# Rounding 64-bit weights to fp32 by an integer addition on GpSimd, in six steps where there were eight, with a new order of the whole program

## The chip, the core and the metric

The kernel runs on one core of a Trainium2 chip. A core has five engines that work side by side, each through its own queue of instructions in a fixed order: TensorE (PE in the profile, with PEld for its weight loads), VectorE (DVE), ScalarE (ACT), GpSimd (POOL) and SyncE (SP, which here only starts transfers). An instruction at the head of a queue that has to wait holds up all that stands behind it. The metric is the time of one execution in microseconds.

## The reference

The program computes attention with pooled queries, and then a feed-forward layer that takes the maximum of three products:

```python
q_pool = q.reshape(B, H, S // 2, 2, D).mean(axis=3)          # q, k, v: (8, 8, 1152, 64)
scores = np.matmul(q_pool, k.transpose(0, 1, 3, 2)) / np.sqrt(D)
scores = scores - np.max(scores, axis=-1, keepdims=True)
attn = np.exp(scores)
attn = attn / (np.sum(attn, axis=-1, keepdims=True) + 1e-09)
x = np.matmul(attn, v).transpose(0, 2, 1, 3).reshape(4608, 512)
h = np.maximum(np.maximum(x @ w1, x @ w2), x @ w3)           # w1, w2, w3: (512, 768)
out = h @ w_out                                              # w_out: (768, 512)
```

The four weight matrices arrive as 64-bit floats, because a 32-bit array was multiplied by a 64-bit scalar on the host. The engines work with 32 bits, so the kernel has to turn each weight into a pair of 32-bit numbers: a high part that TensorE can take in one pass, and a low part that holds the rest.

## The kernel before, in words

**Attention.** The work is cut into 64 units: eight batches, four pairs of heads, two halves of 288 pooled queries. Of a unit d, PE makes nine blocks of scores (`pqk`, lines 441 and 442, four matmuls each, split in high and low queries). ACT copies each block to SBUF (`s`, line 447), and DVE keeps a running maximum of it (`acc`, lines 453 and 456). PE turns the maximum round (`pmt`, line 489), DVE reduces it (`m`, line 495), PE spreads it over the partitions (`pmb`, line 502), DVE subtracts it (line 517), and ACT takes the exponential (line 523). POOL adds up the nine blocks of the exponential (`ksum`, lines 536 and 538). PE multiplies by the values (`pav`, line 556) and sums over the keys (`psum`). A reciprocal (DVE, line 577) and a product (POOL line 580, `xr`) normalise. ACT and POOL then split the result into `xh` and `xl` (lines 644 and 647). For the keys and queries, POOL does the preparation (lines 323, 330, 337).

**Feed-forward.** After the eight units of a batch come 3456 / 8 = 432 matmuls against the three input matrices (`ph`, line 788) and 144 against the output matrix (`po`, line 844). The maximum of three is taken on DVE (`hm`, line 808), and split by ACT and POOL (`h_hi`, `h_lo`). PE runs these matmuls between the attention units of the next batches: they fill it where a unit has to wait.

**Converting the weights.** There are 24 pieces of 128 x 512 weights: 18 for the input matrices, 6 for the output matrix. Each is loaded (line 691) into one of two halves of a buffer `w64` as pairs of 32-bit words, the low word first; so each word is read with a stride of 8 bytes. Eight steps on three engines follow, written as `rebias` to `total` (lines 693 to 725): ACT rebuilds the exponent, DVE puts the sign and upper bits together in two steps, DVE takes out the power of two and scales the low word with it in two more, ACT rounds to the high part, POOL subtracts it, and POOL adds the scaled low word. A piece waits for the buffer half that the piece two before it used; the single scratch tile `w_m` goes from one piece to the next when the step `rest` is done. The converted weights of the input matrices are also stored for the later batches (line 728). The first batch's `ph` needs the 18 pieces one after the other; its first `po` needs all 24, and all of `h_hi` and `h_lo` (the list `hdone`, line 853).

**The order.** Every step is put on a list with its engine, an estimated cost, what it depends on, and an urgency. `arrange` (line 106) then plays the list through with these costs, and takes on each engine the ready step with the lowest urgency. The urgency is the number of the unit plus an entry of the table `RANK` for the kind of step. The result is written out as the fixed order of each engine's queue, so the table and the costs decide only the order.

## Time and profile before

| what | value |
|---|---|
| median of 3 runs | 1508.67 us (1505.15 to 1516.34) |
| the profiled execution: span, first to last instruction (the page has no other time of it) | 1509.3 us |
| PE busy | 1437.4 us, 95% |
| POOL busy | 1133.2 us, 75% |
| DVE busy | 1085.3 us, 72% |
| ACT busy | 912.7 us, 60% |
| conversions, first to last instruction | 57 to 459 us |

The profile gives one execution. Its groups of instructions show the line of the kernel, the engine, the operation, the tiles (output, then inputs), the shape, the count, the busy time with the mean of one in ns, and then how long the engine was idle before them and who ended that. The ends of matmuls are modelled and overlap, so for PE a stretch with many matmuls in a row is a better price than the mean of one. `PEclk` is the clock that TensorE was granted, as a share of its full clock.

### The profile page before, as it was taken

Reading aid. Unit: us, or ns where it says so; the run is one execution under the profiler, and the core shown is the slowest. Engines: PE = TensorE matmul, PEld = TensorE weight load, DVE = VectorE, ACT = ScalarE, POOL = GpSimd, SP = SyncE. Lnnn points to the kernel's source line nnn. Section 1 sums busy time; section 2 is a strip of 40 time slices with the busy share of each in tenths; the row PEclk is TensorE's granted clock in tenths of the full one; section 3 lists DMA queues with packets and bytes.
Section 4 is the critical chain, followed back from the end, with each engine's and each line's share of the span. In section 5 each row is a group of like instructions: output and inputs, shape, how many; then the busy total and the mean of one; then the engine's idle time right before and its main releaser. Section 6 shows DMA issues by size and latency. Waiting matters only on the chain.

```text
span 1509.3 us, 28532 instructions
## 1 busy us (share of the span) xinstructions
PE 1437.4 (95%) x10640; PEld 1234.1 (82%) x10640; DVE 1085.3 (72%) x1417; ACT 912.7 (60%) x1508; POOL 1133.2 (75%) x867
## 2 busy tenths in 40 slices
PE   7889898989679999999999999999999999999999
PEld 6566676777448999898988888888888988889899
DVE  4889789999897754676668776877578776877310
ACT  4766666775566644565666665776566665666311
POOL 1899899998988547667978787887888787885610
PEclk7878999999869999999999999999999999999999
DMA  6565455565544554456545654565555664562141
GB/s 185 145 176 157 111 166 155 162 197 174 173 112 116 171 165 159 132 163 178 162 139 166 194 183 110 164 192 152 153 150 157 189 189 122 164 178 84 61 163 64
DMA packets 105273, 231.51 MB, mean 153 GB/s; under 512 B 14384, under 2 KB 80816, under 8 KB 95920
## 3 DMA queue, kind: packets, MB, share of 16 engines
q1 hardware_dynamic: 104560, 229.11, 51.7%
q8 instruction: 85, 1.39, 0.4%
q10 hardware_dynamic: 576, 0.59, 0.2%
q14 instruction: 52, 0.43, 0.1%
HBM read 135.27 MB, written 18.87 MB: 102 GB/s over the span
## 4 chain that ended last, share of the span: by engine, by line
PE 66%; POOL 2%; DVE 2%; DMA 1%; issue 1%; ACT 1%; SPq 0%; ACTq 0%; POOLq 0%; DVEq 0%
PE ph L788 26%; PE pav L556 12%; PE po L844 10%; PE pqk L441 7%; PE pqk L442 7%; PE pmt L489 2%; PE psum L570 2%; PE pmb L502 1%; POOL ksum L538 1%; DMA qq<-qraw 1%; POOL xl L647 0%; DVE acc L456 0%; ACT s L447 0%; DMA kraw<-in_kT_dram 0%; DVE w L702 0%
## 5 line engine op out<-in xcount | busy, mean ns | idle before, releaser
L538 POOL TENSOR_TENSOR ksum<-ksum,s 128x576 f32<-128x576 f32 x448 | 650.5, 1452 | 29.6 <-ACT s L523 6.6
L788 PE MATMUL ph<-xh,w 128*128 128x288 f32 x2304 | 532.1, 300 | 11.1 <-DVE hm L808 10.2
L447 ACT COPY s<-pqk 128x576 f32<-128x576 f32 x576 | 361.3, 638 | 127.1 <-PE pqk L442 116.1
L517 DVE TENSOR_TENSOR s<-s,pmb 128x864 f32<-128x864 f32 x384 | 394.4, 1045 | 37.4 <-PE pmb L502 37.3
L788 PEld LDWEIGHTS ph<-xh,w 128*128 128x128 f32 x2304 | 392.7, 189 | 20.4 <-DVE hm L808 12.3
L441 PE MATMUL pqk<-qq,kc 128*128 128x288 f32 x1152 | 358.1, 326 | 40.0 <-DVE acc L456 30.6
L456 DVE TENSOR_TENSOR acc<-acc,pqk 128x576 f32<-128x576 f32 x448 | 334.8, 747 | 85.0 <-ACT s L447 81.7
L523 ACT ACTIVATE s<-s 128x864 f32<-128x864 f32 x384 | 354.4, 929 | 56.7 <-DVE s L517 53.0
L788 PE MATMUL ph<-xl,w 128*128 128x288 f32 x1152 | 341.2, 296 | 0.0
L442 PE MATMUL pqk<-qq,kc 128*128 128x288 f32 x1152 | 333.9, 304 | 0.0
L556 PE MATMUL pav<-s,v 128*64 128x288 f32 x2304 | 308.4, 422 | 0.0
L441 PEld LDWEIGHTS pqk<-qq,kc 128*128 128x128 f32 x1152 | 226.3, 196 | 74.7 <-DVE acc L456 47.1
L556 PEld LDWEIGHTS pav<-s,v 128*64 128x64 f32 x2304 | 167.4, 142 | 120.3 <-issue 17.0
L442 PEld LDWEIGHTS pqk<-qq,kc 128*128 128x128 f32 x1152 | 228.5, 198 | 0.0
L788 PEld LDWEIGHTS ph<-xl,w 128*128 128x128 f32 x1152 | 218.0, 189 | 0.0
L536 POOL TENSOR_TENSOR ksum<-s 128x576 f32<-128x576 f32 x64 | 91.7, 1433 | 105.0 <-ACT s L523 101.3
L819 POOL TENSOR_TENSOR h_lo<-hm,h_hi 128x288 fp32r<-128x288 f32 x96 | 79.1, 827 | 100.4 <-ACT h_hi L816 100.4
L495 DVE TENSOR_REDUCE m<-pmt 96x3 f32<-96x384 f32 x128 | 69.5, 550 | 108.8 <-PE pmt L489 108.6
L808 DVE TENSOR_TENSOR hm<-hm,ph 128x288 f32<-128x288 f32 x192 | 86.1, 449 | 79.0 <-PE ph L788 77.5
L577 DVE RECIPROCAL rs<-rs 128x288 f32<-128x288 f32 (+1 forms) x64 | 96.3, 1505 | 56.5 <-ACT rs L574 54.7
L337 POOL TENSOR_TENSOR kraw<-kraw 128x1152 fp32r<-128x1152 f32 x31 | 83.0, 2678 | 51.3 <-DMA qraw<-in_qT_dram 25.8
L844 PE MATMUL po<-h_hi,wo_hi 128*128 128x288 f32 x384 | 115.9, 302 | 0.0
(55 smaller groups left out, 1467.8 us busy)
## 6 DMA issues: line engine op xcount, KB each, us to landing
w<-w_split SPq DMA_DIRECT2D x63, 1024.0 KB, 5.2
kc<-kraw SPq DMA_DIRECT2D x384, 96.0 KB, 2.3
qq<-qraw SPq DMA_DIRECT2D x252, 144.0 KB, 2.9
v<-in_vr_dram SPq DMA_DIRECT2D x32, 576.0 KB, 3.8
kraw<-in_kT_dram SPq DMA_DIRECT2D x31, 576.0 KB, 4.6
qraw<-in_qT_dram SPq DMA_DIRECT2D x31, 576.0 KB, 4.3
w<-in_win_dram SPq DMA_DIRECT2D x18, 512.0 KB, 6.1
w_split<-w SPq DMA_DIRECT2D x9, 1024.0 KB, 5.0
```

The lines of the kernel that those rows point to most:

```text
L441: nc.tensor.matmul(ps[:, h - hs[0], :QH], w, qq[:, 0, h], start=True, stop=False)
L442: nc.tensor.matmul(ps[:, h - hs[0], :QH], w, qq[:, 1, h], start=False, stop=True)
L447: nc.scalar.copy(o.s[kk // 3][:, kk % 3, slice(*hs)], o.ps[kk, hs][:, :, :QH])
L456: nc.vector.tensor_tensor(acc, acc, ps, op=ALU.max)
L517: nc.vector.tensor_tensor(s, s, o.pb[h][:, None, :QH].broadcast_to([P, 3, QH]), op=ALU.subtract)
L523: nc.scalar.activation(s, s, AF.Exp, scale=SCALE)
L536: vec[e].tensor_tensor(o.ksum, o.s[0][:, 0], x, op=ALU.add)
L538: vec[e].tensor_tensor(o.ksum, o.ksum, x, op=ALU.add)
L556: nc.tensor.matmul(o.pav[64 * h : 64 * h + 64, :QH], pr.v[:, kk, h], o.s[kk // 3][:, kk % 3, h], start=(kk == 0), stop=(kk == NK - 1),)
L577: nc.vector.reciprocal(o.rs, o.rs)
L788: nc.tensor.matmul(t.ps[:, :QH], w[:, a, kk], xx[:, kk, qs], start=(kk == 0 and i == 0), stop=(kk == 3 and i == 2),)
L844: nc.tensor.matmul(t.ps[:, :QH], ww[:, kk, ms], hh[:, kk, qs], start=(kk == 0 and i == 0), stop=(kk == 5 and i == 2),)
```

## The change

A double's upper word holds the sign, the exponent and 20 bits of the mantissa. Its lower word holds 32 more, of which fp32 has room for three. Before, the low word was scaled to its place and kept in full, to be added at the end. Now ACT reduces the low word to its upper three bits, rounded, by a product with 2^-29 into an integer (`third`); DVE assembles the upper word as before (`shift`, `sign`); POOL adds the two as 32-bit integers, so that a carry runs on into the exponent (`join`). This is the weight as fp32. ACT rounds it to the high part (`high`) and POOL subtracts that (`low`), now straight into its place. `power`, `rest` and `total` go. The scratch tile `w_m` is free for the next piece when `sign` is done. Two estimated costs are different, and all 43 entries of the table of ranks are new.

```diff
 RANK = {
-    "qk": -95.970825,
-    "cp": 3.506714,
...
+    "qk": -867.337398,
+    "cp": -1020.701831,
...
-            def power(e):
-                nc.vector.tensor_scalar(w_m.bitcast(U32), o.f, 0xFF800000, None, op0=ALU.bitwise_and)
-
-            def rest(e):
-                nc.vector.scalar_tensor_tensor(o.low.bitcast(F32), o.low, 2.0**-52, w_m, op0=ALU.mult, op1=ALU.mult)
+            def third(e):
+                nc.scalar.activation(o.low, o.low, AF.Copy, scale=2.0**-29)
+
+            def join(e):
+                vec[e].tensor_tensor(o.f, o.f, o.low, op=ALU.add)
...
             def low(e):
-                vec[e].tensor_tensor(o.ff, o.ff, o.hi, op=ALU.subtract)
-
-            def total(e):
-                vec[e].tensor_tensor(o.lo, o.ff, o.low.bitcast(F32), op=ALU.add)
+                vec[e].tensor_tensor(o.lo, o.ff, o.hi, op=ALU.subtract)
...
             a = cstep([("sp", 0.4)], load, [converted[j - 2]] if j > 1 else pairs[1].kmoved, size=512)
+            c = cstep([("act", 0.57)], third, [a])
             a = cstep([("act", 0.57)], rebias, [a, rested.get(j - 1)])
-            a = cstep([("dve", 0.8)], shift, [a])
-            a = cstep([("dve", 1.4)], sign, [a])
+            a = cstep([("dve", 0.75)], shift, [a])
+            a = rested[j] = cstep([("dve", 1.4)], sign, [a])
+            a = cstep([("pool", 1.26)], join, [a, c])
             c = cstep([("act", 0.57)], high, [a] + gone)
-            a = cstep([("dve", 0.85)], power, [a])
-            a = rested[j] = cstep([("dve", 0.85)], rest, [a])
-            c = cstep([("pool", 1.26)], low, [c, a])
-            converted[j] = cstep([("pool", 1.26)], total, [c, a])
+            converted[j] = cstep([("pool", 1.0)], low, [c])
```

In the changed kernel `third` is line 707, `join` line 710, `high` still line 719, `low` line 722, and the lines behind them have numbers lower by four.

The new order is seen best at two places. The first is PE's queue at the first matmul of the first batch's `po`. In the names, the first number behind `pqk` is the unit (counted from 0) and the second the block of scores; `po0_0_0` is the first group of `po` of batch 0. Before:

```order
L502 MATMUL pmb20_0_4320<-ident_94,m20_0_4305 128x96 x3
L502 MATMUL pmb20_1_4329<-ident_94,m20_1_4318 128x96 x3
L441 MATMUL pqk21_3_4336<-qq10_1_4081,kc10_1_3996 128x288
L442 MATMUL pqk21_3_4336<-qq10_1_4081,kc10_1_3996 128x288
L441 MATMUL pqk21_3_4336<-qq10_1_4081,kc10_1_3996 128x288
L442 MATMUL pqk21_3_4336<-qq10_1_4081,kc10_1_3996 128x288
L844 MATMUL po0_0_0_4346<-h_hi0_1674,wo_hi_103 128x288
L844 MATMUL po0_0_0_4346<-h_lo0_1675,wo_hi_103 128x288
```

And in the changed kernel, at the same matmul:

```order
L441 MATMUL pqk19_2_3967<-qq9_1_3737,kc9_0_3467 128x288
L442 MATMUL pqk19_2_3967<-qq9_1_3737,kc9_0_3467 128x288
L441 MATMUL pqk19_2_3967<-qq9_1_3737,kc9_0_3467 128x288
L442 MATMUL pqk19_2_3967<-qq9_1_3737,kc9_0_3467 128x288
L840 MATMUL po0_0_0_3976<-h_hi0_1681,wo_hi_103 128x288
L840 MATMUL po0_0_0_3976<-h_lo0_1682,wo_hi_103 128x288
L840 MATMUL po0_0_0_3976<-h_hi0_1681,wo_lo_104 128x288
```

The first `po` moves from behind block 3 of unit 21 to behind block 2 of unit 19. Counted over PE's whole queue ahead of it, there stand 772 `pqk` matmuls before and 696 now, 360 `pav` and 324, 126 `pmt` and 114, 126 `pmb` and 108, 6 of the `psum` of line 570 and 2, and all 432 `ph` of the batch in both.

The second place is POOL's queue at the last piece of the output matrix (`wo_lo` is its low half, `ksum19` the sum of unit 19's blocks). Before:

```order
L722 TENSOR_TENSOR w64_105<-w64_105,wo_hi_103 128x512
L538 TENSOR_TENSOR ksum19_4206<-ksum19_4206,s19_2_4054 128x576
L580 TENSOR_TENSOR xr_107<-xr_107,rs18_4246 128x288
L538 TENSOR_TENSOR ksum19_4206<-ksum19_4206,s19_2_4054 128x576
L725 TENSOR_TENSOR wo_lo_104<-w64_105 128x512
L538 TENSOR_TENSOR ksum19_4206<-ksum19_4206,s19_2_4054 128x576
L722 TENSOR_TENSOR w64_105<-w64_105,wo_hi_103 128x512
L725 TENSOR_TENSOR wo_lo_104<-w64_105 128x512
L536 TENSOR_TENSOR ksum20_4373<-s20_0_4140 128x576
```

And in the changed kernel:

```order
L710 TENSOR_TENSOR w64_105<-w64_105 128x512
L538 TENSOR_TENSOR ksum17_3860<-ksum17_3860,s17_1_3604 128x576
L722 TENSOR_TENSOR wo_lo_104<-w64_105,wo_hi_103 128x512
L710 TENSOR_TENSOR w64_105<-w64_105 128x512
L538 TENSOR_TENSOR ksum17_3860<-ksum17_3860,s17_1_3604 128x576
L722 TENSOR_TENSOR wo_lo_104<-w64_105,wo_hi_103 128x512
L538 TENSOR_TENSOR ksum17_3860<-ksum17_3860,s17_2_3706 128x576
```

The last piece is finished in the middle of unit 17's sum, where it was finished at the end of unit 19's. In the new order one sum stands between a piece's `join` (line 710) and its `low` (line 722), and in that time ACT has to do `high`. Counted over POOL's queue up to the last step of the last piece, there are 160 steps of sums before (20 of line 536, 140 of line 538) and 141 now (18 and 123), 11 of line 337 and 9, 11 of line 323 and 10, 11 of line 330 and 9, 3 of line 580 and none, 12 `h_lo` and 16 `xl` in both, and 48 steps of conversion in both. Counted over DVE's queue up to the last step of a conversion that ACT's last `high` needs, there are 168 maxima (lines 453 and 456) and 151, 40 of line 495 and 36, 120 of line 517 and 108, 19 of line 577 and 16, and 23 each of lines 707 and 710 that are not there any more. On ACT up to the last `high` there are 189 copies of scores and 172, 120 exponentials and 108, and 24 steps `third` that are new.

More of the change, by code (lines that the diff above doesn't have):

```diff
@@ L34 @@
 RANK = {
-    "qk": -95.970825,
-    "cp": 3.506714,
-    "mx": -112.160269,
-    "rows": -148.312644,
-    "red": 23.466841,
-    "bc": -142.276903,
-    "sub": 99.862451,
-    "exp": -189.653089,
-    "keys": 148.893694,
-    "av": 19.232023,
-    "xcopy": -206.02547,
-    "psum": 18.355097,
-    "eps": -181.047585,
-    "inv": 113.796689,
-    "xm": -22.916262,
-    "load": -43.210932,
-    "prep": 250.679273,
-    "move": 65.149737,
-    "split": -97.511902,
-    "ffn": -47.593054,
-    "rate": 0.801853,
-    "mm": 67.95383,
-    "fetch": -234.19152,
-    "evac": -68.37474,
-    "hhigh": 38.661498,
-    "hlow": -51.844784,
-    "conv": 191.981971,
-    "rate0": 3.325971,
-    "first_qk": 41.083979,
-    "first_cp": -105.959101,
-    "first_mx": 56.619279,
-    "first_sub": 16.712798,
-    "first_exp": 260.515882,
-    "first_keys": -71.869651,
-    "first_av": -60.410117,
-    "first_xcopy": 62.582893,
-    "first_psum": -24.318635,
-    "first_inv": -22.423915,
-    "first_xm": -3.450351,
-    "first_load": -260.256351,
-    "first_prep": 57.308365,
-    "first_move": -123.943607,
-    "first_split": 239.216553,
+    "qk": -867.337398,
+    "cp": -1020.701831,
+    "mx": -50.846032,
+    "rows": -2170.249061,
+    "red": -1970.271541,
+    "bc": -886.869509,
+    "sub": -48.271976,
+    "exp": -431.984861,
+    "keys": 698.07215,
+    "av": 20.89773,
+    "xcopy": -534.99975,
+    "psum": -1688.951079,
+    "eps": -2029.164301,
+    "inv": -1616.629935,
+    "xm": 1.735842,
+    "load": 842.07771,
+    "prep": 910.260987,
+    "move": -979.706926,
+    "split": -453.845754,
+    "ffn": -46.517946,
+    "rate": 0.839773,
+    "mm": 69.352276,
+    "fetch": -16.130968,
+    "evac": -1432.973336,
+    "hhigh": 304.771171,
+    "hlow": 664.388548,
+    "conv": 297.955587,
+    "rate0": 7.822039,
+    "first_qk": 270.235766,
+    "first_cp": -256.862538,
+    "first_mx": 744.663022,
+    "first_sub": 1436.30733,
+    "first_exp": 291.229,
+    "first_keys": 1508.105231,
+    "first_av": -87.174641,
+    "first_xcopy": 563.586725,
+    "first_psum": 726.316903,
+    "first_inv": 110.337379,
+    "first_xm": 482.800536,
+    "first_load": -828.565839,
+    "first_prep": 1745.538476,
+    "first_move": -984.902661,
+    "first_split": -1171.347816,
 }
```

## The prediction

> **What bounds the kernel now.** I read the slices of the page first, for where TensorE isn't full. The two rows are PE's busy share and its granted clock, in tenths, in 40 slices of 37.7 us:
>
> ```profile
> PE   7889898989679999999999999999999999999999
> PEclk7878999999869999999999999999999999999999
> ```
>
> Behind the twelfth slice everything is a 9; ahead of it PE has gaps, and the clock is low there too. The two weakest slices, the 11th and 12th (PE 6 and 7, clock 8 and 6), stand just ahead of that, from 377 to 453 us. So the second view is the instructions in order of time around 458 us, POOL and PE:
>
> ```profile
> 457.60 1.04 POOL L725 TENSOR_TENSOR wo_lo<-w 128x512 fp32r<-128x512 f32 x1
> ...
> 458.51 0.30 PE L844 MATMUL po<-h_hi,wo_hi 128*128 128x288 f32 x1
> ```
>
> POOL's last step of the last weight piece ends at 457.60 + 1.04 = 458.6 (spans on POOL are rough), and the first `po`, which needs all 24 pieces, starts at 458.5. That is the gate. The third view cuts the span there; its columns are the stretch and its length, then busy time of PE, PEld, DVE, ACT, POOL with their counts, clock, DMA share, GB/s:
>
> ```profile
> 49.00:458.50 409.50, 352.38 (x2436) 271.06 (x2436) 366.52 (x477) 266.39 (x417) 371.34 (x261) 0.89 0.55 158
> 458.50:1509.30 1050.80, 1044.95 (x7990) 930.74 (x7988) 695.59 (x906) 623.58 (x1057) 744.39 (x590) 1.00 0.51 151
> ```
>
> Behind the gate PE is busy for 1045.0 of 1050.8 us at full clock: that part is bound by PE's work, and no saving elsewhere shortens it. Ahead of it POOL is busy for 371.3 of 409.5 us (91%) and DVE for 366.5 (90%), and PE idles for 57.1 us. ACT, at 266.4, has room. The chain that ended last says who holds PE up there:
>
> ```profile
> 430.79 3.00 DVE w L702
> ...
> 443.75 1.04 DVE w_m L707
> ...
> 445.45 1.17 DVE w L710
> 446.64 0.64 ACT w_m L694
> ...
> 455.25 0.46 PE pmt L489 x3
> ...
> 468.05 0.64 PE psum L570 x4
> ```
>
> The conversion's DVE steps are on it, two of them those that go. The waits in 49 to 459 us agree (engine, line, what it waited for, us, times, longest):
>
> ```profile
> PEld pqk L441 <- DVE acc L456: 37.3, 47, 2.4
> PE pqk L441 <- DVE acc L456: 24.6, 35, 1.9
> ```
>
> PE waits for DVE's maxima, which stand in one queue with the conversion.
>
> So the time is the gate's time plus PE's work behind it. Of the profiled execution the page shows only its span, 1509.3 us; the median of the runs is 1508.67, 0.04% from it, and I make the sum against the span.
>
> **The change part by part: behind the gate.** In the new order 76 `pqk`, 36 `pav`, 12 `pmt`, 18 `pmb` and 4 `psum` matmuls that stood ahead of the first `po` stand behind it (counted in PE's two queues). The prices, from long stretches of the chain:
>
> ```profile
> 1417.82 4.37 PE pav L556 x36
> ...
> 1429.57 57.35 PE ph L788 x432
> ```
>
> A 288-column matmul takes 57.35 / 432 = 0.133 us, so 76 `pqk` are 10.1. A unit's 18 `pav` are 36 in the trace (two passes), 4.37 us, so two units are 8.7. Four groups of three `pmt` at 0.46 are 1.8; six groups of `pmb`, priced like them, at most 2.8; two units of `psum` at 0.64 are 1.3. Sum 24.7. PE's work behind the gate becomes 1050.8 + 24.7 = 1075.5 us, if PE stays as full there. The conversion, the only thing the change takes from these queues, is over by then. **The gate must come before 458.5 - 24.7 = 433.8 us, or nothing is won.**
>
> **Ahead of the gate: POOL.** Groups of POOL in 49 to 459 us (count, then busy time and mean ns of one):
>
> ```profile
> L538 POOL TENSOR_TENSOR ksum<-ksum,s 128x576 f32<-128x576 f32 x133 | 201.1, 1512 | 11.2 <-ACT s L523 5.1
> L536 POOL TENSOR_TENSOR ksum<-s 128x576 f32<-128x576 f32 x19 | 27.0, 1422 | 14.3 <-ACT s L523 14.2
> L722 POOL TENSOR_TENSOR w<-w,w 128x512 f32<-128x512 f32 x18 | 26.8, 1492 | 0.1
> L337 POOL TENSOR_TENSOR kraw<-kraw 128x1152 fp32r<-128x1152 f32 x10 | 26.7, 2671 | 5.6 <-DMA w<-in_win_dram 5.0 <-ACT kraw L333 0.6
> L725 POOL TENSOR_TENSOR w<-w 128x512 fp32r<-128x512 f32 x18 | 20.5, 1139 | 0.2
> L330 POOL TENSOR_TENSOR qraw<-qraw 128x576 fp32r<-128x576 f32 x10 | 16.2, 1618 | 3.3 <-ACT qraw L326 3.3
> L323 POOL TENSOR_TENSOR qraw<-qraw 128x576 f32<-128x576 f32 x10 | 14.4, 1442 | 1.1 <-DMA qraw<-in_qT_dram 1.1
> L722 POOL TENSOR_TENSOR w<-w,wo_hi 128x512 f32<-128x512 f32 x6 | 8.6, 1436 | 0.4 <-issue 0.4
> L725 POOL TENSOR_TENSOR wo_lo<-w 128x512 fp32r<-128x512 f32 x6 | 7.3, 1218 | 0.2
> L580 POOL TENSOR_TENSOR xr<-xr,rs 128x288 f32<-128x288 f32 x3 | 3.3, 1096 | 0.0
> ```
>
> Up to the last piece POOL has in the new order 17 sums less at 1.512 (25.7 us), 2 first sums at 1.422 (2.8), 2 of line 337 at 2.671 (5.3), 1 of line 323 (1.4), 2 of line 330 (3.2) and 3 of line 580 (3.3): 41.7 us. The conversion has 48 steps on POOL as before. They cost 26.8 + 8.6 + 20.5 + 7.3 = 63.2 us, 2.63 a piece. No row shows an integer addition on POOL. `join` reads and writes with a stride, as line 722 does in part; `low` writes without one, as line 725. Both lie by these rows between 1.14 and 1.49, so the sum moves by -8.5 to +8.4 us; I take one of each, no change. With every other microsecond unchanged the gate is at 458.5 - 41.7 = 416.8.
>
> A second term is the stretch that POOL and DVE cause each other. In 600 to 1400 us, where nothing is converted, the same sum on POOL takes
>
> ```profile
> L538 POOL TENSOR_TENSOR ksum<-ksum,s 128x576 f32<-128x576 f32 x265 | 378.2, 1428 | 15.3 <-ACT s L523 1.5
> ```
>
> 1.428 against 1.512: 133 x 0.084 = 11.2 us. The DVE steps that go swing likewise (min/median/max ns):
>
> ```profile
> L707 DVE TENSOR_SCALAR w_m<-w x24: 381/972/1687, 64.9 to 451.3; 128x512 uint32<-128x512 uint32 x24
> L710 DVE SCALAR_TENSOR_TENSOR w<-w,w_m x24: 693/1238/1807, 65.9 to 452.2; 128x512 f32<-128x512 uint32 x24
> ```
>
> A step of fixed shape that takes 0.38 or 1.69 us is waiting for something inside. Of the conversion's 96 DVE steps 48 stay, so I take half of the 11.2: 6 us (bounds 0 and 11). **Gate at 411.**
>
> The Trainium skill (SBUF — State Buffer, section "SBUF: two separate sides") says that VectorE and GpSimd share a pair of ports as an exclusive lock, taken for the whole instruction, and by VectorE only for operations with two SBUF inputs or in a two-port mode; the swing in the two rows above agrees with it. By that rule alone the relief goes with the steps that take the lock, and all of the conversion's do, so it gives the same half; without it the gate would be at 417 and the time 1492.
>
> **Ahead of the gate: DVE, ACT, PE.** Rows of the whole execution:
>
> ```profile
> L710 DVE SCALAR_TENSOR_TENSOR w<-w,w_m 128x512 f32<-128x512 uint32 x24 | 33.0, 1374 | 0.4
> L707 DVE TENSOR_SCALAR w_m<-w 128x512 uint32<-128x512 uint32 x24 | 24.9, 1038 | 0.3
> L517 DVE TENSOR_TENSOR s<-s,pmb 128x864 f32<-128x864 f32 x384 | 394.4, 1045 | 37.4 <-PE pmb L502 37.3
> L456 DVE TENSOR_TENSOR acc<-acc,pqk 128x576 f32<-128x576 f32 x448 | 334.8, 747 | 85.0 <-ACT s L447 81.7
> L447 ACT COPY s<-pqk 128x576 f32<-128x576 f32 x576 | 361.3, 638 | 127.1 <-PE pqk L442 116.1
> L523 ACT ACTIVATE s<-s 128x864 f32<-128x864 f32 x384 | 354.4, 929 | 56.7 <-DVE s L517 53.0
> L694 ACT ACTIVATE w_m<-w 128x512 f32<-128x512 f32 x24 | 16.3, 681 | 23.6 <-DVE w L710 17.4 <-POOL ksum L538 5.0 <-DMA w<-in_win_dram 1.2
> ```
>
> DVE loses 23 x 1.374 + 23 x 1.038 = 55.5 us of conversion, and by the order 17 maxima (12.7) and 12 subtractions (12.5): over 80 us, twice POOL's 41.7 (which puts DVE's own way to the gate under 378). So DVE, level with POOL before, no longer decides. ACT gets 24 `third`, by line 694's row 0.681 each, 16.3 us, and loses 17 copies (10.8) and 12 exponentials (11.1): 5.6 less. The ACT waits for `w_m` from line 710 (17.4) shorten, since `sign` now frees it; I cost that at nothing, ACT's 143 us of idle time covering it, and at 17 us were ACT full. The DMAs are the same in number and size; their places in SP's queue I cost at nothing, as POOL's rows show one wait for a weight load (5.0 us), and at another 5.0 if it comes twice.
>
> PE has 24.7 us less ahead of the gate, so at its old losses it would be there at 433.8, not at 411: 23 us of its losses must go. Those are 57.1 us idle, and 0.11 of 409.5, 45 us, of clock. The waits for DVE's maxima alone are 37.3 us on the weight loads (I take the 24.6 on the matmuls as the same moments), and the weak slices 11 and 12, where no `ph` is left and no `po` allowed, go when the gate comes earlier. I take it that they give the 23.
>
> **Sum.** 411 + 1075.5 = 1486.5, so 1486 us, 1.5% under the span.
>
> **The rivals.** A: PE keeps its losses. Its waits come from the round of copy, maximum and next block, which the change leaves; then the gate is at 425 to 440 and the time about 1509 (433.8 + 1075.5). For it: PE waits for a maximum, and not for a conversion step itself; against it: DVE at 90% now has a fifth less to do, and in the chain above the conversion's steps stand between the maxima. This is also how the change could do nothing it says: the steps saved were no one's wait.
>
> B: more comes than I count. POOL's 38.2 us of idle time are waits for ACT's exponentials, which wait for DVE; halved, the gate is at 392 and the time 1467.
>
> C: `join` is slow. If the integer path takes twice line 722's 1.49, 24 x 1.49 = 36 us more, and no stretch relief: gate 453, time 1528. It breaks even at 24 x 0.95 on top, a `join` of about 2.4 us. The Trainium skill (GPSIMD Engine Reference, section 4.1 "Engine selection") says that GpSimd adds 32-bit integers natively and exactly; no run here shows a duration, so it only lowers this chance.
>
> D, the other side by a new wait: POOL was asked for two steps in a row, with 0.9 us of idle time ahead of all 48 (the last figures of the four rows); now `low` waits for ACT's `high`, which waits for `join`, with one sum between. ACT's queue holds copies and exponentials there; if each of the 48 steps finds POOL waiting for one 0.93 us exponential, that is 45 us: gate 456, time 1531. Behind the blocked POOL stand the sums, and PE's `psum` waits for them. It breaks even from 23 / 48 = 0.5 us a step. For it: POOL is the fullest engine. Against it: a sum covers 1.5 us, and ACT has a third of its time free.
>
> **How the numbers follow.** A measurement of this kernel can tell about 1% (15 us) from no change. Forecast 0.50 (1475 to 1498, by the bounds of POOL's steps and of the stretch), B 0.12, A 0.20, D 0.11, C 0.07. Faster by over 1% is under 1494: B and seven eighths of the forecast, 0.56. Slower, over 1524: most of D and C, 0.14. The rest, 0.30, is A and the edges. The range leaves out the end of B below and the far ends of C and D above: 1460 to 1521. The forecast's own is 1475 to 1498.
>
> **What would show it.** First `po` near 411 us with units 19 to 21 behind it; PE over 99% busy from there; POOL's sums ahead of it nearer 1.47; `join` and `low` together near 2.6 us; PE's waits for line 456 ahead of the gate down by 20 us. It is wrong if the gate comes after 430 (A, or D if POOL idles ahead of line 722 for over 10 us, or C if line 710 is over 2.4), or if PE has gaps behind it: each 0.1 us in the 45 units behind it is 4.5 us.

## The result and the profile after

The changed kernel takes 1465.39 us (median of 4 runs, 1464.28 to 1467.21) against 1509.22 (4 runs, 1505.15 to 1516.34): a ratio of 0.971, 95% interval 0.968 to 0.974. The forecast was 1486. Sign and range (1460 to 1521) hold; the time lies outside the forecast's own 1475 to 1498, and the gain is 44 us where 23 were forecast.

The profiled execution has a span of 1465.4 us. PE's busy share and granted clock in 40 slices of 36.6 us:

```profile
PE   7789899999899999999999999999999999999999
PEclk7989899999899999999999999999999999999999
```

The weak slices 11 and 12 of before (PE 6 and 7, clock 8 and 6) are gone; one 8 is left of them. The instructions in order of time around the first `po`, POOL and PE:

```profile
396.26 1.04 POOL L710 TENSOR_TENSOR w<-w 128x512 uint32<-128x512 uint32 x1
...
397.92 0.29 PE L840 MATMUL po<-h_hi,wo_hi 128*128 128x288 f32 x1
...
398.66 1.29 POOL L722 TENSOR_TENSOR wo_lo<-w,wo_hi 128x512 fp32r<-128x512 f32 x1
```

The first `po` is at 397.92, and POOL's last step of the last piece begins 0.7 us behind it. So the gate isn't a wait for that step. The busy time of each engine in the stretches around the gate (columns as in the prediction; the first two rows are before's and after's first 49 us, the others after's):

```profile
0.00:49.00 49.00, 40.07 (x218) 32.30 (x219) 23.15 (x35) 22.71 (x35) 17.45 (x17) 0.79 0.64 169
```

```profile
0.00:49.00 49.00, 37.02 (x200) 30.32 (x200) 22.15 (x33) 21.34 (x32) 15.45 (x16) 0.79 0.60 158
49.00:397.92 348.92, 309.58 (x2269) 244.57 (x2267) 288.36 (x393) 253.12 (x406) 319.12 (x235) 0.92 0.59 172
397.92:1465.40 1067.48, 1062.91 (x8176) 949.07 (x8174) 726.44 (x944) 652.88 (x1096) 785.39 (x618) 1.00 0.51 153
```

The gate comes 60.6 us earlier, and 16.7 us more stand behind it (1067.5 for 1050.8): 43.9 us. Behind it PE is 99.6% busy (99.4% before). Ahead of it POOL is busy 319.1 of 348.9 us (91%, as before), DVE only 288.4 (83%, before 90%). Groups of POOL and of the conversion in after, in the 349 us ahead of the gate:

```profile
L538 POOL TENSOR_TENSOR ksum<-ksum,s 128x576 f32<-128x576 f32 x118 | 173.3, 1470 | 7.6 <-ACT s L523 3.7
L702 DVE SCALAR_TENSOR_TENSOR w<-w_m,w 128x512 uint32<-128x512 uint32 x24 | 36.3, 1511 | 0.5
L710 POOL TENSOR_TENSOR w<-w 128x512 uint32<-128x512 uint32 x24 | 26.8, 1117 | 1.3 <-DVE w L702 1.3
L722 POOL TENSOR_TENSOR w<-w,w 128x512 fp32r<-128x512 f32 x18 | 25.2, 1404 | 1.7 <-ACT w L719 1.7
L707 ACT ACTIVATE w<-w 128x512 uint32<-128x512 uint32 x24 | 16.7, 696 | 3.9 <-DMA w<-in_win_dram 3.9
```

`join` takes 1.12 us and `low` 1.40: 2.52 a piece for 2.63. POOL idles 1.7 us in all ahead of `low` in the input matrices. And the waits in that stretch (engine, line, what it waited for, us, times, longest):

```profile
PEld pqk L441 <- DVE acc L456: 18.3, 24, 3.2
PE pqk L441 <- DVE acc L456: 16.2, 20, 2.9
ACT w L719 <- POOL w L710: 13.8, 9, 3.5
...
PEld psum L587 <- POOL ksum L538: 6.3, 7, 1.5
...
PEld pmb L502 <- DVE m L495: 4.2, 7, 1.8
```

PE's wait for DVE's maxima is halved (37.3 to 18.3 us on the weight loads). ACT waits 13.8 us for `join`, a new wait. The chain that ended last, from 326 us on, shows who sets the pace now:

```profile
326.47 1.48 POOL ksum L538
328.03 1.74 POOL ksum L538
...
332.74 1.33 POOL w L722
334.07 1.00 POOL w L710
335.07 0.78 POOL ksum L538
336.43 1.32 POOL w L722
```

Here POOL's steps follow each other. The chain of before has such a row too (nine POOL steps, from 415.7 to 429.2 us), but beside it DVE's conversion steps, of which this stretch of after has none.

### The profile page after: what moved, and what is told of

Read it like the earlier page. It is cut to its first block, busy times and chain, and to the rows that moved or that the text cites. A ratio compares the mean times of both kernels' runs of the same rounds, so it can differ in the third digit from the quotient of the medians.

```text
span 1465.4 us, 28407 instructions
## 1 busy us (share of the span) xinstructions
PE 1409.5 (96%) x10640; PEld 1224.0 (84%) x10640; DVE 1036.9 (71%) x1369; ACT 927.3 (63%) x1532; POOL 1120.0 (76%) x867
## 4 chain that ended last, share of the span: by engine, by line
PE 77%; POOL 9%; issue 4%; ACT 4%; DVE 4%; DMA 2%; SPq 1%; POOLq 0%; ACTq 0%; DVEq 0%
PE ph L784 27%; PE pav L556 16%; PE po L840 10%; PE pqk L441 8%; PE pqk L442 8%; POOL ksum L538 5%; PE pmt L489 3%; PE psum L570 2%; PE pmb L502 2%; DVE acc L456 1%; ACT s L447 1%; ACT s L523 1%; DVE s L517 1%; POOL w L710 1%; POOL w L722 1%
## 5 line engine op out<-in xcount | busy, mean ns | idle before, releaser
L784 PE MATMUL ph<-xh,w 128*128 128x288 f32 x2304 | 525.6, 298 | 3.4 <-DVE hm L804 2.8
L447 ACT COPY s<-pqk 128x576 f32<-128x576 f32 x576 | 365.3, 638 | 129.1 <-PE pqk L442 113.4
L784 PEld LDWEIGHTS ph<-xh,w 128*128 128x128 f32 x2304 | 389.8, 188 | 10.3 <-issue 5.7
L441 PE MATMUL pqk<-qq,kc 128*128 128x288 f32 x1152 | 349.5, 318 | 33.4 <-DVE acc L456 25.9
L442 PE MATMUL pqk<-qq,kc 128*128 128x288 f32 x1152 | 329.7, 301 | 0.0
L441 PEld LDWEIGHTS pqk<-qq,kc 128*128 128x128 f32 x1152 | 223.0, 194 | 57.0 <-DVE acc L456 33.0
L556 PEld LDWEIGHTS pav<-s,v 128*64 128x64 f32 x2304 | 167.4, 140 | 119.0 <-issue 12.9
L442 PEld LDWEIGHTS pqk<-qq,kc 128*128 128x128 f32 x1152 | 224.5, 195 | 0.0
```

Of the source, the lines that this page charges most:

```text
L441: nc.tensor.matmul(ps[:, h - hs[0], :QH], w, qq[:, 0, h], start=True, stop=False)
L442: nc.tensor.matmul(ps[:, h - hs[0], :QH], w, qq[:, 1, h], start=False, stop=True)
L447: nc.scalar.copy(o.s[kk // 3][:, kk % 3, slice(*hs)], o.ps[kk, hs][:, :, :QH])
L556: nc.tensor.matmul(o.pav[64 * h : 64 * h + 64, :QH], pr.v[:, kk, h], o.s[kk // 3][:, kk % 3, h], start=(kk == 0), stop=(kk == NK - 1),)
L784: nc.tensor.matmul(t.ps[:, :QH], w[:, a, kk], xx[:, kk, qs], start=(kk == 0 and i == 0), stop=(kk == 3 and i == 2),)
```

## The experiments

Three readings had to be told apart. **One**: POOL's work sets the gate, and the new order puts less of it there; the DVE steps that go matter little. **Two**: DVE sets it as well, by the sheer time of the steps that go, or by what they do to POOL. **Three**: one half of the change, conversion or table, makes the whole gain.

All of this is read from the stretch from 49 us to the first `po`. Each kernel's window gives its length and the busy time of DVE and POOL in it; idle is the length less that. In a fence of an experiment the line numbers are its own, some higher than after's by the lines it adds. Each ratio is against the kernel before, run beside it (medians 1509.5 to 1511.3). The theories that an expectation names are those of its own text.

| kernel | median us | first po at | behind it | DVE busy, idle | POOL busy, idle |
|---|---|---|---|---|---|
| before | 1509.2 | 458.5 | 1050.8 | 366.5, 43.0 | 371.3, 38.2 |
| after | 1465.4 | 397.9 | 1067.5 | 288.4, 60.6 | 319.1, 29.8 |
| e1: new conversion, old table | 1505.1 | 450.1 | 1053.2 | 313.2, 87.9 | 358.0, 43.1 |
| e2: old conversion, new table | 1524.9 | 477.1 | 1048.6 | 363.9, 64.2 | 368.1, 60.0 |
| e3: after, two DVE steps more on a piece's own data | 1503.9 | 432.3 | 1066.7 | 333.1, 50.2 | 330.0, 53.3 |
| e4: after, one POOL step more | 1485.7 | 418.4 | 1069.0 | 290.8, 78.6 | 338.8, 30.7 |
| e5: after, two reductions more | 1469.8 | 397.5 | 1067.0 | 309.5, 39.0 | 320.3, 28.2 |
| e6: after, the two removed kinds of step again, on constants | 1508.9 | 442.4 | 1065.8 | 343.2, 50.2 | 332.2, 61.2 |
| e8: new conversion, old table but one entry | 1492.2 | 425.9 | 1063.9 | 297.9, 79.0 | 338.8, 38.1 |
| e9: after, one entry old | 1468.2 | 390.3 | 1078.0 | 278.6, 62.7 | 312.0, 29.3 |
| e11: after, four reductions more | 1498.9 | 432.0 | 1066.6 | 336.3, 46.7 | 320.4, 62.6 |
| e12: before without the two DVE steps | 1496.4 | 442.9 | 1052.1 | 314.9, 79.0 | 359.3, 34.6 |
| e13: after without `sign` | 1453.6 | 383.9 | 1068.1 | 254.6, 80.3 | 308.1, 26.9 |
| e14: after, a third of `low` on DVE | 1459.6 | 390.3 | 1066.9 | 287.2, 54.1 | 312.9, 28.4 |

One of e5's four runs took 2275 us, at a granted clock of 0.554 where the other three have 0.970 to 0.976; those three lie within 1466.2 to 1470.4, and e5's median and ratio are theirs.

### The two halves alone (e1, e2)

e1 has the new conversion with its dependences and estimated costs, and the old table; e2 the old conversion with the new table. Their core:

```diff
# e1: before, and
+            c = cstep([("act", 0.57)], third, [a])
...
+            a = rested[j] = cstep([("dve", 1.4)], sign, [a])
+            a = cstep([("pool", 1.26)], join, [a, c])
...
+            converted[j] = cstep([("pool", 1.0)], low, [c])
# e2: before, and
-    "keys": 148.893694,
+    "keys": 698.07215,
...
```

> The new six-step conversion and its costs, but the table of ranks of before; the first po stands in PE's queue behind 768 pqk matmuls, as before (772). Theory 1 (the steps saved on DVE and the stretch of POOL count by themselves, the order only puts less ahead of the first po): first po near 445 us, time about 1495 us, PE's work behind the first po about 1050 us. Theory 2 (the new table made the whole gain): time within 5 us of 1509. Theory 3 (the conversion made the whole gain): 1465 to 1472.

> The eight-step conversion of before with the new table of ranks; the first po stands behind 772 pqk matmuls, as before. Theory 1: no step is saved, so first po near 455 us and, if the new order fills PE better behind it (a batch took 168 us before and 166 in the changed kernel), a time of about 1500 us. Theory 2 (the new table made the whole gain): 1465 to 1475. Theory 3 (the conversion made the whole gain): 1509 within 5.

e1: ratio 0.996 (0.994 to 0.998). e2: 1.009 (1.008 to 1.011). By its time alone e1 lies within the 5 us of 1509 that the theory of the table asks for, but by that theory e2 would take 1465 to 1475, and it is slower than before; so none of the three fits both runs. Neither half makes the gain, and they do not add up to it: -6 and +14 us apart, against the kernel before beside them (1511.2), and -44 together. The windows ahead of the gate, of e1 and of e2:

```profile
49.00:450.10 401.10, 345.77 (x2443) 267.99 (x2441) 313.18 (x430) 277.37 (x442) 358.00 (x261) 0.89 0.56 161
```

```profile
49.00:477.10 428.10, 353.84 (x2437) 274.67 (x2436) 363.94 (x477) 269.04 (x417) 368.06 (x259) 0.88 0.52 150
```

In e1 DVE is busy 53 us less than before, but POOL only 13 less, and the gate moves by 8. In e2 the table, played through with the old conversion's steps, puts the first `po` behind 772 `pqk` as before, not behind 696, so the kernel doesn't have after's order. The order is made by table and steps together, and the two can't be taken apart by swapping the table. The next runs keep after's order and change one engine's load in it.

### POOL's load in the new order (e4)

A second integer addition on POOL for each piece, into a tile that nobody reads:

```diff
             def join(e):
                 vec[e].tensor_tensor(o.f, o.f, o.low, op=ALU.add)
+                vec[e].tensor_tensor(w_d.bitcast(U32), o.low, o.low, op=ALU.add)
```

> The changed kernel in its own order, with a second integer addition on POOL behind each join, written to a tile that nobody reads: 24 x 1.12 = 27 us more on POOL ahead of the first po. Theory 1 (POOL paces the way to the first po, 91% busy): first po 20 to 27 us later, time 1485 to 1492 us. Rival (PE's round of copy, maximum and next block paces, POOL has slack): under 8 us more.

Measured 1485.65 us, 0.984 (0.982 to 0.985), as reading one expected. The added steps and POOL's window:

```profile
L712 POOL TENSOR_TENSOR w_d<-w 128x512 uint32<-128x512 uint32 x23 | 26.9, 1170 | 0.0
```

```profile
49.00:418.40 369.40, 318.21 (x2257) 251.41 (x2256) 290.82 (x393) 252.18 (x403) 338.75 (x255) 0.89 0.56 161
```

POOL's busy time ahead of the gate rises by 19.6 us (319.1 to 338.8) and the gate moves by 20.5. Not all of the 26.9 us of additions shows there, since two sums and a `join` that stood in after's stretch fall outside this one, and `low` is shorter (1.31 us for 1.40). POOL's idle time stays at 30. What PE waits for changes too:

```profile
PEld psum L588 <- POOL ksum L539: 21.1, 13, 3.6
```

PE's wait for POOL's sums goes from 6.3 to 21.1 us. In the new order, with DVE's load as after has it, POOL paces, one for one.

### DVE's load in the new order (e3, e5, e6, e11)

e3 puts two steps of the removed kind behind `sign`, on the piece's own data:

```diff
             def sign(e):
...
+                nc.vector.tensor_scalar(w_d.bitcast(U32), o.f, 0xFF800000, None, op0=ALU.bitwise_and)
+                nc.vector.scalar_tensor_tensor(w_d, w_d, 2.0**-52, w_m, op0=ALU.mult, op1=ALU.mult)
```

> The changed kernel in its own order, with two further DVE steps per piece, of the forms of power and rest, written to a tile that nobody reads. They put 24 x 2.4 = 58 us back on DVE, and two operations per piece that POOL shares its ports with. Theory 1 (DVE had to be relieved before POOL could pace): DVE would be busy for 346 of the 349 us between 49 and the first po, so the first po moves by 20 to 45 us and the time is 1485 to 1510. Rival (the order alone moved the first po, DVE's steps were no one's wait): under 5 us more, 1465 to 1470.

Measured 1503.89 us, 0.995 (0.993 to 0.997), in the range expected, but not for one reason alone: these steps read what `join` writes, so POOL waits 10.3 us for them, a wait that neither kernel has. `join` also takes 1.521 us, for 1.117 in after, while the sums stay at 1.465.

```profile
L713 POOL TENSOR_TENSOR w<-w 128x512 uint32<-128x512 uint32 x24 | 36.5, 1521 | 13.5 <-DVE w_d L706 10.3 <-ACT kraw L334 1.6 <-ACT xr L566 0.4
```

e5, e11 and e6 are without that: their steps read a constant tile and write one that nobody reads. e5 adds two reductions (one input), e11 four, e6 the two removed kinds of step.

```diff
             def sign(e):
...
# e5, and e11 with range(4)
+                for i in range(2):
+                    nc.vector.tensor_reduce(w_e[:, i : i + 1], w_d, axis=AX.X, op=ALU.max)
# e6
+                nc.vector.tensor_scalar(w_e.bitcast(U32), w_d.bitcast(U32), 0xFF800000, None, op0=ALU.bitwise_and)
+                nc.vector.scalar_tensor_tensor(w_e, w_d, 2.0**-52, w_d, op0=ALU.mult, op1=ALU.mult)
```

> The changed kernel in its own order, with two reductions of a constant 128x512 tile on DVE per piece, right behind sign. Nobody reads their result, they hold nothing that another step waits for, and they have one SBUF input. By the 0.55 us of the reduction of line 495 they are some 1.2 us a piece, 29 us on DVE ahead of the first po. The run before with two further steps moved the first po by 34 us, but those read tiles that join and the next rebias had to wait for. Theory 1a (DVE's time itself is on PE's path): first po 10 to 25 us later, time 1476 to 1492. Theory 1b (what cost was POOL's stretch and the waits of join and rebias, not DVE's time): under 6 us more.

> As the run above, but the two DVE steps have the forms of the removed power and rest (a tensor_scalar, and a scalar_tensor_tensor with two SBUF inputs) on constant tiles, 0.38 + 0.69 = 1.07 us a piece where nothing disturbs them (the shortest of before). Theory 1b: the steps stretch to over 2 us a piece, POOL's sums ahead of the first po become longer by some 0.04 us each and the first po moves by 10 to 20 us, time 1476 to 1488. Theory 1a: the same as the run above within 5 us.

> The changed kernel in its own order, with four reductions of a constant tile per piece on DVE where the run with reductions had two: 24 x 4 x 0.67 = 65 us of DVE time, as much as the two steps with the forms of power and rest took (62.2 us, gate 44 us later). Theory 2 (such a step costs because it waits inside DVE for POOL's running instruction, and makes POOL wait, not by DVE's time): the first po moves by under 20 us, time under 1487; what it moves by comes from DVE being 97% busy. Rival (DVE's time alone, past some 90%): first po 35 to 50 us later, time 1500 to 1515.

e5: 0.972 (0.967 to 0.977), the gate where after has it. The added group and the window:

```profile
L709 DVE TENSOR_REDUCE w_e<-w_d 128x1 f32<-128x512 f32 x48 | 30.4, 672 | 0.0
```

```profile
49.00:397.50 348.50, 308.78 (x2244) 245.40 (x2244) 309.51 (x442) 251.57 (x403) 320.28 (x236) 0.91 0.59 170
```

30.4 us of additional steps on DVE cost nothing that the runs can tell (0.972 for after's 0.971). From this alone the removed 55 us on DVE would look worthless, and what was left was that those steps do harm by what they share with POOL. e6 seemed to bear that out: 0.998 (0.996 to 1.000), so the whole gain is gone, which neither of its expectations had.

```profile
L709 DVE SCALAR_TENSOR_TENSOR w_e<-w_d 128x512 f32<-128x512 f32 x24 | 35.3, 1469 | 0.8
L708 DVE TENSOR_SCALAR w_e<-w_d 128x512 uint32<-128x512 uint32 x24 | 26.9, 1121 | 0.0
```

But e6 also adds 62.2 us to DVE, twice what e5 adds. e11 matches that with 58.9 us of reductions:

```profile
L709 DVE TENSOR_REDUCE w_e<-w_d 128x1 f32<-128x512 f32 x96 | 58.9, 671 | 0.0
```

```profile
49.00:432.00 383.00, 324.21 (x2269) 259.25 (x2268) 336.27 (x493) 254.72 (x406) 320.43 (x238) 0.87 0.53 156
```

e11: 0.991 (0.989 to 0.994), the gate at 432.0, 34.1 us later than after's and a little short of what its rival expected. So the theory that only sharing matters falls: POOL is busy there for 320.4 us as in e5, but idles for 62.6, not 28.2. Of the time added to DVE the first 30 us are free and the next 28.5 cost 34.5 us. e6 comes 10.4 us later than e11. POOL is busy 11.7 us longer there (the sums 6.7, `join` 5.1), but DVE is busy 6.9 us longer too, so how much of the 10.4 is POOL's stretch is not separated. It is at most the smaller part of the 44.5 us that e6 adds to after. PE's waits in e6 and e11, the same line:

```profile
PEld pmb L505 <- DVE m L498: 32.4, 12, 4.7
```

```profile
PEld pmb L505 <- DVE m L498: 27.6, 11, 4.6
```

In after it is 4.2 us and in e5 12.3: DVE holds PE now. The table says where one engine takes over from the other. Where POOL paces in the new order (after, e4, e5, e9, e13, e14) it idles for 27 to 31 us. With more load on DVE, POOL's idle time doubles to 53 to 63 (e3, e6, e11), while DVE's own idle time doesn't fall below the 39 us of e5 (47 to 50). DVE's busy share would not have told: it is 89% in e5, which costs nothing, and 88% in e11. All these runs put the added steps in one block behind `sign`, and DVE takes its steps in order; whether the cost is in DVE's total time or in a block of 2.7 us that holds up the step PE waits for was not tested.

### Relief of DVE in the old order, and more of it in the new (e12, e13)

e12 is the kernel before without `power` and `rest`; e13 is the changed kernel without `sign`.

```diff
# e12
             def power(e):
-                nc.vector.tensor_scalar(w_m.bitcast(U32), o.f, 0xFF800000, None, op0=ALU.bitwise_and)
+                pass
...
             def rest(e):
-                nc.vector.scalar_tensor_tensor(o.low.bitcast(F32), o.low, 2.0**-52, w_m, op0=ALU.mult, op1=ALU.mult)
+                pass
...
             def total(e):
-                vec[e].tensor_tensor(o.lo, o.ff, o.low.bitcast(F32), op=ALU.add)
+                vec[e].tensor_tensor(o.lo, o.ff, o.ff, op=ALU.add)
# e13
             def sign(e):
-                nc.vector.scalar_tensor_tensor(
-                    o.f, w_m.bitcast(U32), 0x80000000, o.f, op0=ALU.bitwise_and, op1=ALU.bitwise_or
-                )
+                pass
```

> The kernel before in its own order, with power and rest left out, so that the low word is not scaled; POOL's last addition adds the rest of the high word to itself instead. The weights' low parts are therefore not those of the reference. Theory 2 (the two steps that share POOL's ports are the cost, whatever the order): first po 25 to 45 us earlier than in the kernel before, time 1465 to 1485. Rival (the steps saved pay only with the new order, as the run with the new conversion and the old table suggested, 1505): first po under 12 us earlier, time over 1497.

> The changed kernel in its own order, with the step sign left out, so that all weights lose their sign. That is one more of the DVE steps with two SBUF inputs gone, 36.3 us of DVE time (1.51 us each). Theory 2: the first po comes 8 to 25 us earlier, time 1440 to 1457, since POOL stretches less and DVE is not held. Rival (POOL paces alone now): 0 to 6 us earlier, 1459 to 1465.

e12: 0.990 (0.988 to 0.993), the gate 15.6 us earlier, between the two expectations. e13: 0.962 (0.959 to 0.965), the gate 14.0 earlier than after's, as expected.

```profile
49.00:442.90 393.90, 343.77 (x2457) 267.15 (x2454) 314.91 (x432) 267.26 (x419) 359.28 (x262) 0.91 0.58 165
```

```profile
49.00:383.90 334.90, 304.53 (x2256) 243.66 (x2255) 254.58 (x369) 250.35 (x403) 308.05 (x234) 0.92 0.62 178
```

In e12 DVE is relieved of 51.6 us, POOL of 12.1 (14.4 counted from the span's start), by steps that are stretched less and by a `total` that reads other operands, and the gate follows POOL. So does most of e13's: by e5 DVE was in nobody's way there, yet without `sign` POOL is busy 11.1 us less in the stretch (9.4 from the span's start, as one sum now stands ahead of 49 us). Its sums take 1.437 us, for 1.470 in after:

```profile
L538 POOL TENSOR_TENSOR ksum<-ksum,s 128x576 f32<-128x576 f32 x117 | 167.9, 1437 | 7.7 <-ACT s L523 3.8
```

With e6 this makes a square, though not an exact one: e6's steps work on constants, and e12's `total` has other operands. With the DVE steps: 1509 in the old order, 1509 in the new (e6). Without them: 1496 in the old (e12), 1465 in the new. The new order is worth nothing while DVE has these steps, for then DVE holds PE. The steps' removal is worth 13 us in the old order, about what POOL's work gets shorter by it; that DVE's time paced in the old order is not shown. Together they are worth 44. So reading three falls. Reading one is right that POOL sets the gate of after, and wrong that the DVE steps matter little: POOL can set it in the new order because DVE was relieved, as reading two has it.

### The order (e8, e9)

e8 is the new conversion with the old table, but for the rank of the sums (`keys`), which now come behind conversions on POOL. e9 is the changed kernel with the old rank of the conversion.

```diff
# e8: e1, and
-    "keys": 148.893694,
+    "keys": 698.07215,
# e9: after, and
-    "conv": 297.955587,
+    "conv": 191.981971,
```

> The new conversion with the old table, but for one entry: the rank of POOL's sums is the new table's, 698 for 149, so that POOL takes a conversion step ahead of a sum whenever both are ready. In PE's queue the first po then stands behind 740 pqk matmuls (768 with the old table, 696 with the new), and 0.94 of the batch's ph stand ahead of unit 18 (0.70 and 1.00). Theory 1 (the saved steps pay if the order lets the conversion go ahead): first po near 425 us, time 1480 to 1490. Rival (the table's gain is in many entries together): over 1495.

> The changed kernel with one entry of its table set back, the rank of the conversion (192 for 298). The first po stands behind 672 pqk matmuls, where it stood behind 696. Theory 1: what stands less ahead stands more behind, and the first po comes earlier by what POOL has less to do up to it, some 6 sums and a preparation, 10 us, against 8 us more behind: time 1458 to 1468. Rival (POOL and DVE do not get there sooner, PE waits): 1470 to 1480.

e8: 0.989 (0.984 to 0.994), 12.9 us under e1. It is nearer to the expectation that POOL's order makes the difference (1480 to 1490) than to the other, but outside it. By this one entry the first `po` stands behind 740 `pqk` (768 in e1, 696 in after), POOL has 19.2 us less to do ahead of it, and the gate comes 24.2 earlier. It is a third of the way from e1 to after; the other entries make the rest. e9: 0.972 (0.968 to 0.976), 1468.2 us, at the upper edge of what was expected. The gate comes 7.6 us earlier than after's, behind 672 `pqk`, and 10.5 us more stand behind it: this step further along the same way wins nothing.

### A third of `low` on DVE (e14)

If POOL paces one for one, and DVE has some 20 us free, a third of `low` is better on DVE:

```diff
             def low(e):
-                vec[e].tensor_tensor(o.lo, o.ff, o.hi, op=ALU.subtract)
+                (nc.vector if j % 3 == 2 else vec[e]).tensor_tensor(o.lo, o.ff, o.hi, op=ALU.subtract)
```

> The changed kernel, with `low` of every third piece (8 of 24) on DVE instead of POOL; nothing else differs, and 696 pqk still stand ahead of the first po. Theory: POOL paces the way to the first po one for one, and DVE's time there is free up to about 310 of 349 us (so two reductions a piece, 30 us, cost nothing). POOL loses 8 x 1.40 = 11 us, DVE gains 8 x about 1.4 = 11 us and stands at about 300 us: the first po comes 8 to 11 us earlier, at 387 to 390, and the time is 1454 to 1459 us. Rival: DVE, which takes its steps in order, is held at `low` until ACT's `high` is done, and the sums behind it with it, or `low` on DVE stretches POOL as the removed steps did: the first po comes at 395 or later and the time is 1463 to 1480 us.

Measured 1459.62 us, 0.966 (0.964 to 0.968); against after, which ran at another time, 5.8 us less, with intervals of the ratio that just touch. That it is faster than after is likely, but no run beside after shows it.

```profile
49.00:390.27 341.27, 306.95 (x2256) 244.31 (x2256) 287.19 (x400) 251.87 (x404) 312.92 (x227) 0.92 0.60 175
```

```profile
L538 POOL TENSOR_TENSOR ksum<-ksum,s 128x576 f32<-128x576 f32 x117 | 175.1, 1498 | 8.5 <-ACT s L523 4.2
...
L722 DVE TENSOR_TENSOR w<-w,w 128x512 fp32r<-128x512 f32 x6 | 6.0, 1002 | 0.2 <-ACT w L719 0.2
```

The gate comes 7.6 us earlier and POOL is busy 6.2 us less, not the 11 of the eight steps: only seven of them stood ahead of after's gate (9.8 us), and the sums beside the two-input steps on DVE go from 1.470 to 1.498 us, 3.3 us over 117. Gate and time lie just outside the expectation (390.3 us for 387 to 390, 1459.6 for 1454 to 1459).

## Why the prediction was right, and where it was off

**What bounds the kernel.** The time is the gate and PE's work behind it in all fourteen profiles: PE idles 3.6 to 8.0 us behind it in every one. The step that the gate is POOL's last step of the last piece was wrong: in after that step ends behind the first `po`. The list `hdone` only makes `arrange` place the first `po` behind all 24 pieces. The matmul itself reads the first of the output matrix's six pieces alone, and POOL began the last step of that one at 354.8 us. POOL and PE come there side by side because the fixed queues, and the waits between them, keep them together; what moves the gate is POOL's whole work ahead of it (e4, e13), as long as DVE does not hold PE (e6, e11).

**POOL ahead of the gate.** Forecast -47.7 us of busy time (41.7 by counts, 6 of stretch). By the windows from the start it is (15.45 + 319.12) - (17.45 + 371.34) = -54.2. The counted terms were right: over the same time the group of line 538 loses 30.7 us by its busy time, where 25.7 + 6 were forecast.

```profile
L538 POOL TENSOR_TENSOR ksum<-ksum,s 128x576 f32<-128x576 f32 x140 | 211.1, 1508 | 11.8 <-ACT s L523 5.1
```

```profile
L538 POOL TENSOR_TENSOR ksum<-ksum,s 128x576 f32<-128x576 f32 x123 | 180.4, 1468 | 8.0 <-ACT s L523 3.7
```

Half the stretch was the right choice: 1.470 for the forecast's 1.47. The runs bear out that the stretch goes with the DVE steps: 1.478 in the old order without two of them (e12), 1.437 without a third in the new (e13), 1.521 with two put back (e6). Only in e3, with two put back, it is `join` that is longer and not the sums. Mis-sized was the conversion, taken as unchanged: 1.117 + 1.404 a piece are 60.5 us for 24, 2.7 less, and the last 1.3 of them stand behind the gate.

**POOL's idle time.** The sum left it as it was; in the stretch ahead of the gate it fell by 8.4 us (38.2 to 29.8), most of it ahead of the first sums, which wait for ACT's exponentials (14.2 us before, 8.2 now):

```profile
L536 POOL TENSOR_TENSOR ksum<-s 128x576 f32<-128x576 f32 x17 | 24.3, 1432 | 8.2 <-ACT s L523 8.2
```

This was rival B's mechanism, with less than half of its 19 us. B had called all 38.2 us such waits; by the prediction's own rows 19.3 were (14.2 and 5.1). With the busy time, and 2.0 us more idle time in the first 49 us, it makes the gate's 60.6: the gate stands at 397.9 where 411 was forecast.

**DVE no longer decides.** Right, but the prediction gave the DVE steps that go no price of their own, other than the stretch. e6 and e11 show one: put back into the new order, such load takes the whole gain (e6) or most of it (e11), and there PE waits for DVE. The break-even is closer than the prediction's "a fifth less to do" makes it: some 30 us of after's relief were to spare (e5), and with 59 us put back in the same place most of the gain was gone (e11).

**PE's losses ahead of the gate.** 23 us had to go; 35 did. Idle time fell from 57.1 to 39.3 us and the clock's share from 45.0 to 0.08 of 348.9, 27.9 us. Rival A, which kept them, is out. The waits for line 456 fell by 19.0 us, where 20 were named, but not for the reason given, that DVE's maxima stand in one queue with the conversion. In the old order they stay when DVE is relieved (38.1 us in e1, 42.5 in e12), and in the new order they stay low when its load is put back (21.2 in e11, 22.0 in e6). e12 and e6:

```profile
PEld pqk L441 <- DVE acc L456: 42.5, 46, 3.1
```

```profile
PEld pqk L444 <- DVE acc L459: 22.0, 24, 4.2
```

So this wait goes with the order, and the number named was met by luck. Rival A's premise, that the wait comes from the round of copy, maximum and next block, fits this better; what A missed is that the new order changes the round.

**Behind the gate.** Forecast +24.7, measured +16.7. The matmuls moved there are those counted, but PE does the same work in less: 1044.95 + 24.7 would be 1069.7 us busy, and it is 1062.9. The first `po` of two batches in a row, in before and in after:

```profile
902.09 0.40 PE L844 MATMUL po<-h_hi,wo_hi 128*128 128x288 f32 x1
...
1069.65 0.40 PE L844 MATMUL po<-h_hi,wo_hi 128*128 128x288 f32 x1
```

```profile
873.86 0.40 PE L840 MATMUL po<-h_hi,wo_hi 128*128 128x288 f32 x1
...
1039.64 0.40 PE L840 MATMUL po<-h_hi,wo_hi 128*128 128x288 f32 x1
```

A batch takes 167.6 us in the old order and 165.8 in the new, and three such batches in a row stand behind the gate in both: some 5.4 of the 8.0 us. It is the order and not the conversion: a batch takes 167.4 us in e1, with the new conversion and the old table, and 165.8 in e2, with the old conversion and the new table. The same batch in before and in after:

```profile
902.09:1069.65 167.56, 166.91 (x1282) 146.29 (x1280) 124.39 (x160) 110.55 (x184) 133.86 (x105) 1.00 0.57 165
```

```profile
873.86:1039.64 165.78, 165.78 (x1283) 146.29 (x1281) 124.52 (x161) 111.43 (x184) 134.07 (x105) 1.00 0.57 165
```

PE idles for 0.65 us in before and not at all in after. The idle time shows only part of a wait here: a matmul's modelled span is about 0.30 us, and the next one starts 0.133 us later, so up to 0.16 us of a wait counts as busy. From start to start, before's two waits in this batch, at 946.5 and 1013.8 us, come to 0.96 us. The other 0.8 us of a batch, and the 2.6 us outside the three batches, stay open.

**Rivals C and D.** `join` takes 1.12 us, not 2.4, and POOL idles 1.7 us ahead of `low` and not 45. The hand-off's wait is on ACT, 13.8 us at `high`, where there was room.

In sum, of the 21 us between forecast and span, 13 lie ahead of the gate (6.5 of POOL's busy time, 6.4 of its idle time) and 8 behind it. The mechanism of the sum holds, with three terms mis-sized, all to the same side. That the time, 1465, is near rival B's 1467, which had a chance of 0.12, is a coincidence: B put all of it into POOL's idle time.

**Open.** e2's gate comes 18.6 us later than before's, though no engine has more than 3 us more work ahead of it: DVE and POOL both idle for 60 us and more, and PE waits for DVE's maxima as long as before.

```profile
PEld pqk L441 <- DVE acc L456: 38.0, 34, 6.0
```

The order was made for other steps; which place of it costs the time was not tried.

## What to carry to other kernels

Where two engines are both 90% busy ahead of a gate, what a relief of one is worth depends on the other: measure it by adding load to each in the final order, and look at whose idle time grows. The engine that paces keeps its own (POOL's 27 to 31 us); when another takes over, it grows (53 to 63 us). A planner's table belongs to the steps it was found for: with other steps it gives another order, and swapping it alone tests neither. Load added as twice a small dose tells a free engine from one that is only just not pacing.

## What the runs showed of the hardware

An integer addition of 128x512 words on POOL, all three operands with a stride of 8 bytes, takes 1.117 us on average (1.04 in the row shown), less than an fp32 subtraction of the same size that writes without a stride (1.40 us). That does not make integers faster: before's fp32 addition of line 725 takes 1.03 us at the shortest, as `join` does. The prediction's bounds were 1.14 to 1.49.

Reductions of 128x512 on DVE take 0.67 us each, 48 or 96 of them, beside a POOL that is over 80% busy, and leave POOL's sums at 1.475 and 1.464 us. The two steps of e6, 0.38 and 0.69 us at the shortest in before, take 1.12 and 1.47 us there on average, and the sums 1.521. The sums of e5, e11 and e6:

```profile
L541 POOL TENSOR_TENSOR ksum<-ksum,s 128x576 f32<-128x576 f32 x117 | 172.4, 1475 | 6.1 <-ACT s L526 2.5
```

```profile
L541 POOL TENSOR_TENSOR ksum<-ksum,s 128x576 f32<-128x576 f32 x119 | 174.1, 1464 | 7.1 <-ACT s L526 3.3
```

```profile
L541 POOL TENSOR_TENSOR ksum<-ksum,s 128x576 f32<-128x576 f32 x119 | 180.8, 1521 | 8.7 <-ACT s L526 4.9
```

The Trainium skill (SBUF — State Buffer, section "SBUF: two separate sides") says that VectorE takes the pair of ports it shares with GpSimd for operations with two SBUF inputs or in a two-port mode, and the loser blocks for the whole instruction. The runs agree for the reductions, which have one input. e6's first step has one input too and is stretched all the same; that fits only if it runs in a two-port mode. Its shortest time in before, 0.38 us where a reduction of the same 128x512 takes 0.67, would go with a faster mode, but no run here shows the mode.

What the stretch costs is mostly not POOL's time. e6's two steps would take 26 us on DVE at their shortest, and 30 us of reductions were free there (e5); stretched they take 62.2 us, and the gate comes 44.5 us later, of which POOL's longer steps (13.0 us more busy time than in after) can explain the smaller part at most.
